# Two short score units in one set of PSUM banks, the product with v in two tasks, and a new order

## The chip, the cores and the metric

The kernel runs on 1 core of one Trainium2 chip. The metric is the device time of one execution in microseconds (us). TensorE (PE) multiplies and transposes into PSUM, VectorE (DVE), ScalarE (ACT) and GpSimd (POOL) do elementwise work, SyncE (SP) issues most DMAs. PSUM is handled here as eight banks of 512 fp32 columns.

## The reference

The inputs are q, k, v of shape (8 batches, 8 heads, 576, 64), a decay f of (8, 8, 576), and an MLP with w1 (512 x 1024) and w2 (1024 x 512), capacity 128.

```
scores = q k^T / 8 + cum[i] - cum[j],  cum = cumsum(log(clip(f)))   # causal
attn   = softmax(scores);  x = attn v, the heads side by side: (8, 576, 512)
per batch: s = x . w_gate;  the 128 rows with the highest s:
   out[row] = x[row] + sigmoid(s[row]) * (relu(x[row] w1) w2);  other rows: out = x
```

## The kernel before

**Pairs and units.** The 64 heads are worked in 32 pairs. q and k are split into a rounded fp32r part and its rest (`rounded`, `rest`), so that the scores are three products; a fourth adds the decay. The causal scores of a pair fall into five units: units 0 to 3 are blocks of 128 queries of either head against 128, 256, 384 and 512 keys, and unit 4 holds the last 64 queries of both heads against all 576. For each unit there is a score task on PE (`s`, line 667, or `s4`, line 735), a mask with a running minimum on DVE (`m`, lines 687, 739), an exponential on ACT (`ex`, lines 692, 747), a turn by 64 x 64 transposes on PE (`tr`, through `turn`, line 352) and two copies of the turned block into `pt` (`cp`; line 335 on ACT, 337 on DVE). A score task takes two banks, one for each head, and a turn task two. Score products and transposes of 64 rows go two at a time, one on the upper and one on the lower rows of the array.

**Product with v.** When all ten copies of a pair are there, one PE task (`av_all`, line 792) runs six pieces, each for both heads, into two neighbouring banks, and one copy of 576 columns takes them to `ot`. `back` turns `ot` (line 352 again, two banks), `norm` divides (line 844), `gate` and `fold` on POOL prepare the gate score (lines 850, 856).

**MLP.** When a batch's gate scores are complete, DVE ranks them (line 999), the 128 rows are gathered by an indirect DMA (line 1054), `xg` (line 1091) forms their gate product again and `xp` turns them; then come the two products (lines 1141, 1182, 1189, 1234, 1242) and a scatter (line 1253). Six of the eight batches are worked two at a time.

**Order.** All tasks are given to a planner (`Flow`) that holds a cost for each and writes the instruction order of every engine. Of the tasks that are ready it takes, on an engine, those whose start lies within `EPS` of the earliest, and among them the one with the smallest `place`, a due time, plus `GW` times the gap that PE is held to need between kinds of tasks. A task with a choice of engines goes where it would end first, with `BD` added for DVE. Tokens stand for buffers; a token "ps" is one bank, or two neighbours. Instructions keep the planned order on their engine, and semaphores order the engines.

```
tks = [Token("ps") for _ in range(2)]          # scores of a unit
tk_t = Token("ps", 2, wide=2)                  # turn of a unit
tk_ot, tk_av = Token("ot", 1), Token("ps", wide=2)
d_xg = add({"dve": 0.7}, xg, after=[q["got"]], place=tx, take=[tk_x])
d_xp = add(turns(ND) ..., xp, after=[d_xg, d_ident], place=tx, ...)
```

Of the kernel before, what the change touches and what calls it, by code (L numbers as in the profile page):

```python
# [17 lines left out]
P = 128  # L18
# [17 lines left out]
class Flow:  # L36
# [18 lines left out]
    def __init__(self, slots, eps, bias, weight, eps0):  # L55
# [122 lines left out]
def kernel(  # L178
# [36 lines left out]
    BD = 0.46  # L215
# [7 lines left out]
    GW = 49.43  # L223
    EPS = 0.05
    EPS0 = 0.21
# [22 lines left out]
    WN = 1  # L248
    Z2 = 2.12
# [3 lines left out]
    OR = 1  # L253
    ORDER = ((3, 0, 2, 1, 4), (4, 3, 0, 2, 1), (3, 2, 4, 1, 0), (3, 2, 1, 0, 4), (0, 3, 2, 1, 4), (4, 3, 2, 1, 0))[OR]
# [25 lines left out]
    sel = const.tile([P, NPAIR], F32R, name="sel")  # L280
    blk = const.tile([P, P], F32, name="blk")
# [93 lines left out]
    def turns(n):  # L375
# [4 lines left out]
                 "oh": 1, "gs": 2}, EPS, {"dve": BD}, GW, EPS0)  # L380
# [154 lines left out]

    def pair_load(p):
# [21 lines left out]
        come = [load(t_b, 295, after=pads, place=pl, take=[tk])]  # L558
        return come + [load(t_a, 295, 3, after=pads + come, place=pl + 0.01)], tk
# [3 lines left out]
    def split_parts(p, come, tk):  # L563
# [24 lines left out]
        if p < HELP1:  # L588
# [3 lines left out]
            rq = part(c1, rounded(qs), after=ready, place=pl)  # L592
            rk = part(c1, rounded(ks), after=ready, place=pl + 0.01)
            lq = part(c2, rest(qs), after=[rq], place=pl + 0.03)
            lk = part(c2, rest(ks), after=[rk], place=pl + 0.04)
# [14 lines left out]
        d_bm[p] = add({"pool": 0.6}, t_bm, after=[d_blk, d_sel] + used4.get(p - 2, []), place=pl)  # L610
# [11 lines left out]
    def pair_parts(p):  # L622
# [13 lines left out]
        lv = load(t_v, 288, 2, rate=300, after=([d_ep] if p == 1 else []) + [d_more[1]] + avd[p - 2:p - 1] * (p > 1), place=9 * p - PV, take=[tk_v])  # L636
# [7 lines left out]
        for u, i in enumerate(ORDER if p else (*(i for i in ORDER if i < NF), NF)):  # L644
            t = 9 * p + 2 * u
            ahead = moved[-LOOK:][:1] if len(moved) >= LOOK else []
            tl = t - LP
            if i < NF:
                n = (i + 1) * P
# [4 lines left out]
                def s(e, k, i=i, n=n, tks=tks, scs=scs, pss=pss):  # L654
                    for par in range(2):
                        if k == 0:
                            scs[par] = bank(tks[par])
                            pss[par] = pw.tile([P, n], F32, tag=f"p{i}", name=f"p{p}_{i}_{par}", bufs=NB[i])
                    cs = [q_cols(p, par, i) for par in range(2)]
                    for m_ in ((0,), (1,), (2,), (3,))[k]:  # L660
                        for par in range(2):
                            h_ = HALVES[par]
                            if m_ == 3:
                                lt, rt = sel[h_, p:p + 1].broadcast_to([R, P]), ep[h_, 0:n]
                            else:
                                lt, rt = q_part(p, m_ == 1)[h_, cs[par]], k_part(p, m_ == 2)[h_, 0:n]
                            nc.tensor.matmul(scs[par][:, :n], lt, rt, start=m_ == 0, stop=m_ == 3)  # L667

                one = max(n / 2400 + 0.014, 0.107) + 0.01
                if p < SPLIT:  # L670
# [3 lines left out]
                    for k in range(4):  # L674
                        x2 = add({"pe": one}, lambda e, k=k, s=s: s(e, k), after=deps[k] + [x2] + (ahead if k == 0 else []),
                                 place=tl + 0.02 * k, take=tks + tks_p if k == 0 else [], kind="score")
                else:
                    x2 = add({"pe": 4 * one}, lambda e, s=s: [s(e, k) for k in range(4)], after=ops[p][0] + ops[p][1] + ahead,
                             place=tl, take=tks + tks_p, kind="score")
                used[p].append(x2)  # L680
                x4s = []
                for par in range(2):
                    tk_nm = Token("nm")

                    def m(e, par=par, n=n, i=i, scs=scs, pss=pss, nms=nms):
                        nm = nms[par] = small.tile([P, 1], F32, tag="nm", name=f"nm{p}_{i}_{par}", bufs=6)
                        nc.vector.tensor_tensor_reduce(  # L687
                            out=pss[par], in0=scs[par][:, :n], in1=mask[:, 512 - n:512], scale=-0.125, scalar=BIG,
                            op0=ALU.add, op1=ALU.min, accum_out=nm)

                    def ex(e, par=par, i=i, pss=pss, nms=nms):
                        nc.scalar.activation(pss[par], pss[par], AF.Exp, bias=nms[par], scale=-1.0,  # L692
                                             accum_out=sts[p % 3][:, i, par:par + 1])

                    x3 = add({"dve": n / 960 + 0.15}, m, after=[x2, d_mask], place=tl + PM + 0.05 * par, take=[tk_nm], give=[tks[par]])
                    x4s.append(add({"act": n / 1200 + 0.295}, ex, after=[x3, d_sums] + d_more[0:1] + invs[p - 3:p - 2] * (p > 2),
                                   place=tl + PE_ + 0.05 * par, give=[tk_nm]))
                sums += x4s
                tk_t = Token("ps", 2, wide=2)

                def tr(e, i=i, tk_t=tk_t, pss=pss):
                    for par in range(2):
                        for j in range(i + 1):
                            turn(tk_t, par * (i + 1) + (j if par == 0 else i - j), pss[par][:, j * P:(j + 1) * P])

                def cp(e, par, i=i, tk_t=tk_t):
# [3 lines left out]
                    copy_on(e, d_, turned(tk_t, par * (i + 1), i + 1))  # L710

                x5 = add(turns(2 * (i + 1)), tr, after=x4s + [d_pt, d_ident], place=t, take=[tk_t], give=tks_p, kind="turn")
                for par in range(2):
                    copied.append(add({**act(n), **dve(n)}, lambda e, par=par, cp=cp: cp(e, par), after=[x5],
                                      place=t + PC + 0.1 * par, give=[tk_t]))
            else:
# [28 lines left out]
                def ex(e):  # L745
# [4 lines left out]
                         take=[tk_b, tk_p], kind="full")  # L750
                used[p].append(x2)
                used4[p] = [x2]
                x3 = add({"dve": S / 960 + 0.15}, m, after=[x2, d_mask4, d_blank], place=tl + U4 + PM, take=[tk_nm], give=[tk_b])
                x4 = add({"act": S / 1200 + 0.295}, ex, after=[x3, d_sums] + d_more[0:1] + invs[p - 3:p - 2] * (p > 2),
                         place=tl + U4 + PE_, give=[tk_nm])
# [13 lines left out]
                x5 = add(turns(NCH), tr, after=[x4, d_pt, d_ident], place=t, take=[tk_t], give=[tk_p], kind="turn")  # L769
                for k in range(2):  # L770
                    w = NCH * R
                    copied.append(add({**act(w), **dve(w)}, lambda e, k=k, cp=cp: cp(e, k), after=[x5],
                                      place=t + PC + 0.1 * k, give=[tk_t]))
# [5 lines left out]
        pieces = ((0, 1), (1, 1), (0, 0), (2, 1), (4, 1), (3, 1))  # L779
        tk_ot, tk_av = Token("ot", 1), Token("ps", wide=2)  # L780
        avs = []
        for n, (j, g) in enumerate(pieces):
            q0 = max(j * P, g * SPL)
            q1 = SPL if g == 0 else S

            def av(e, n=n, j=j, g=g, q0=q0, q1=q1):
                if n == 0:
                    avb[0] = bank(tk_av)
                vt, pt = vts[p], pts[p]
                for par in range(2):  # L790
                    off = (640 * j if par == 0 else 2624 - 512 * j) + q0 - j * P
                    nc.tensor.matmul(  # L792
                        avb[0][par * D:(par + 1) * D, 512 - SPL + q0:512 - SPL + q1],
                        vt[:, j, par * D:(par + 1) * D], pt[:, off:off + q1 - q0],
                        start=(j == 0), stop=(g == 0 or n == len(pieces) - 1))

            avs.append((av, 4 * (q1 - q0)))

        def av_all(e):
            for fn, _ in avs:  # L800
                fn(e)

        x5 = add({"pe": sum(c for _, c in avs) / 2400 + 0.1}, av_all, after=copied + [lv],
                 place=9 * (p + 1) + VO, take=[tk_ot, tk_av], give=[tk_pt, tk_v], kind="av")
        avd.append(x5)

        def out(e):
            copy_on(e, ot[:, 0:S], avb[0][:, 512 - SPL:512 - SPL + S])

# [528 lines left out]
```

## Time and profile before

| | |
|---|---|
| median of 3 runs | 442.49 us (441.96 to 443.34) |
| profiled execution | 440.93 us, its span 439.1 us |
| PE clock granted | 1.00 |
| busy: PE, DVE, ACT, POOL | 400.4, 315.7, 305.0, 278.0 us |

The span runs from the first to the last instruction of the profiled execution. Busy time is the union of an engine's instructions; the ends of matmuls are modelled, so a busy PE is not PE at its peak. "Idle before" in a line is the time in which the engine had nothing to do just ahead of those instructions, and the arrow names what ended it.

### The profile page before, as it was taken

To read this page: it belongs to the slowest core of one execution; us is meant where nothing else is said; L and a number is where in the kernel's file an instruction comes from. 1 tells how busy PE (TensorE), PEld (TensorE's weight loads), DVE (VectorE), ACT (ScalarE), POOL (GpSimd) and SP (SyncE) were. 2 spreads that over 40 slices of the span, in tenths; PEclk is the share of its full clock that TensorE was granted. 3 is DMA by queue.
4 is the path that set the end of the run, shared out by engine and by line. 5 is a ranking of instruction groups with operands and counts; after the bars stand their busy time and mean duration, and the time that the engine had idled before them with its cause. 6 is when DMAs were issued, how large, how long until landed. Compare 5 with 4: busy or idle time off the path is not lost.

```text
span 439.1 us, 12615 instructions
## 1 busy us (share of the span) xinstructions
PE 400.4 (91%) x4649; PEld 317.3 (72%) x4649; DVE 315.7 (72%) x1212; ACT 305.0 (69%) x942; POOL 278.0 (63%) x264
## 2 busy tenths in 40 slices
PE   1999989999889999999999999999999999899995
PEld 1777667777667777798776897777767777698774
DVE  6777777987788876975786738676679787788511
ACT  4799999999889896840588830688879788611310
POOL 4499989999848867952378721568876883310201
PEclk9999999999999999999999999999999999999999
DMA  7965555826443527442134430153536222210201
GB/s 182 269 171 157 134 158 149 222 60 186 125 126 82 160 62 215 139 109 78 52 113 130 137 85 24 52 159 84 150 96 171 80 84 85 53 50 30 73 0 48
DMA packets 43699, 49.82 MB, mean 113 GB/s; under 512 B 6163, under 2 KB 33846, under 8 KB 43638
## 3 DMA queue, kind: packets, MB, share of 16 engines
q1 hardware_dynamic: 42278, 44.68, 36.8%
q0 software_dynamic: 1280, 4.20, 2.9%
q8 instruction: 36, 0.59, 0.6%
q14 instruction: 25, 0.20, 0.2%
q10 hardware_dynamic: 80, 0.15, 0.1%
HBM read 37.45 MB, written 11.55 MB: 112 GB/s over the span
## 4 chain that ended last, share of the span: by engine, by line
ACT 39%; PE 28%; DVE 17%; issue 10%; POOL 2%; DMA 2%; SPq 1%; POOLq 0%; ACTq 0%; DVEq 0%
ACT p L692 20%; ACT pt L335 10%; PE psum L1141 8%; PE psum L667 5%; DVE p L687 5%; PE psum L792 5%; ACT p L747 4%; DVE pt L337 4%; PE psum L1234 4%; DVE j L999 3%; ACT ot L335 3%; PE psum L352 3%; DVE x L844 2%; PE psum L735 2%; PE psum L1242 2%
## 5 line engine op out<-in xcount | busy, mean ns | idle before, releaser
L692 ACT ACTIVATE p<-p,nm 128x512 f32<-128x512 f32 (+3 forms) x256 | 141.1, 559 | 30.9 <-DVE nm L687 30.8
L687 DVE CUSTOM_DVE_ANT_0 p<-psum,mask 128x512 f32<-128x512 f32 (+3 forms) x256 | 110.3, 486 | 7.6 <-PE psum L667 4.1
L667 PE MATMUL psum<-op 64*128 64x512 f32 (+3 forms) x768 | 89.3, 335 | 12.0 <-ACT op L335 9.5
L792 PE MATMUL psum<-pt,v 128*64 128x448 f32 (+4 forms) x768 | 93.8, 393 | 0.2 <-ACT pt L335 0.2
L335 ACT COPY pt<-psum 128x128 f32<-128x128 f32 (+4 forms) x264 | 91.3, 445 | 2.5 <-PE psum L352 2.4
L584 POOL TENSOR_TENSOR op<-raw,op 128x1216 fp32r<-128x1216 f32 (+2 forms) x41 | 88.4, 2165 | 3.0 <-ACT op L335 2.9
L850 POOL TENSOR_TENSOR gp<-x,wg 128x640 f32<-128x640 f32 x31 | 48.9, 1578 | 48.9 <-DVE x L844 46.8
L667 PEld LDWEIGHTS psum<-op 64*128 64x128 f32 x768 | 66.7, 190 | 17.1 <-ACT op L335 9.5
L352 PE MATMUL psum<-ident,p 64*128 64x64 f32 x1600 | 69.3, 228 | 8.3 <-ACT p L747 2.7
L792 PEld LDWEIGHTS psum<-pt,v 128*64 128x64 f32 x768 | 45.4, 137 | 42.9 <-issue 27.8
L352 PEld LDWEIGHTS psum<-ident,p 64*128 64x128 f32 x1600 | 59.4, 139 | 23.4 <-ACT p L692 6.0
L999 DVE TENSOR_SCALAR_CACHE_REDUCE j<-srow,sg 128x128 uint8<-128x128 f32 (+5 forms) x107 | 53.3, 498 | 3.9 <-ACT srow L978 1.3
L337 DVE COPY pt<-psum 128x512 f32<-128x512 f32 (+4 forms) x56 | 27.3, 508 | 35.5 <-ACT pt L335 29.2
L692 ACT ACTIVATION_READ_ACCUMULATOR p<-p,nm 128x1 f32 x256 | 49.9, 195 | 0.0
L856 POOL TENSOR_TENSOR gp<-gp 128x320 f32<-128x320 f32 (+1 forms) x62 | 43.5, 702 | 4.0
L667 PE MATMUL psum<-ep,sel 64*128 64x512 f32 (+3 forms) x256 | 45.0, 324 | 0.0
L577 POOL TENSOR_SCALAR op<-raw 128x1216 fp32r<-128x1216 f32 (+2 forms) x32 | 33.1, 1034 | 7.8 <-PE psum L735 7.3
L335 ACT COPY ot<-psum 128x576 f32<-128x576 f32 x32 | 20.1, 628 | 24.1 <-PE psum L792 24.1
L735 PE MATMUL psum<-op 128*128 128x288 f32 x192 | 34.0, 312 | 1.5 <-DVE nm L687 1.2
L1253 POOL DMA_INDIRECT out_dram<-xe,idx x8 | 8.3, 1034 | 39.2 <-DVE xe L1249 31.0
L735 PEld LDWEIGHTS psum<-op 128*128 128x128 f32 x192 | 26.6, 188 | 5.8 <-DVE nm L687 2.7
L739 DVE CUSTOM_DVE_ANT_0 p<-psum,mask 128x576 f32<-128x576 f32 x32 | 24.2, 756 | 6.5 <-PE psum L735 3.0
(121 smaller groups left out, 597.8 us busy)
## 6 DMA issues: line engine op xcount, KB each, us to landing
raw<-in_qk_dram SPq DMA_DIRECT2D x31, 288.0 KB, 5.4
v<-in_v_dram SPq DMA_DIRECT2D x32, 256.0 KB, 3.0
out_dram<-x SPq DMA_DIRECT2D x16, 512.0 KB, 3.3
raw<-in_qk_dram SPq DMA_DIRECT2D x31, 144.0 KB, 3.3
raw<-in_qk_dram SPq DMA_DIRECT2D x31, 128.0 KB, 3.9
srow<-sd SPq DMA_DIRECT2D x7, 320.0 KB, 4.3
wst<-in_w_dram SPq DMA_DIRECT2D x4, 512.0 KB, 6.6
wst<-in_w_dram SPq DMA_DIRECT2D x8, 256.0 KB, 4.5
```

The costliest lines, as they stand in the source:

```text
L335: nc.scalar.copy(d, s_)
L337: nc.vector.tensor_copy(d, s_)
L352: nc.tensor.transpose(psum[:, o:o + R], src[k_], ident[k_, k_])
L584: (nc.vector if e == "dve" else nc.gpsimd).tensor_tensor(op[:, 1, cs], raw[:, cs], op[:, 0, cs].bitcast(F32), ALU.subtract)
L667: nc.tensor.matmul(scs[par][:, :n], lt, rt, start=m_ == 0, stop=m_ == 3)
L687: nc.vector.tensor_tensor_reduce(out=pss[par], in0=scs[par][:, :n], in1=mask[:, 512 - n:512], scale=-0.125, scalar=BIG, op0=ALU.add, op1=A ...
L692: nc.scalar.activation(pss[par], pss[par], AF.Exp, bias=nms[par], scale=-1.0, accum_out=sts[p % 3][:, i, par:par + 1])
L735: nc.tensor.matmul(sc[:, g * 512:g * 512 + HALF], lt, rt, start=m_ == 0, stop=m_ == 3)
L792: nc.tensor.matmul(avb[0][par * D:(par + 1) * D, 512 - SPL + q0:512 - SPL + q1], vt[:, j, par * D:(par + 1) * D], pt[:, off:off + q1 - q0] ...
L850: (nc.vector if e == "dve" else nc.gpsimd).tensor_tensor(out=st["gp"], in0=x_part(), in1=wg[:, hp * P:(hp + 1) * P].unsqueeze(1).broadcast ...
L856: nc.gpsimd.tensor_tensor(out=g_[:, :, 0:w], in0=g_[:, :, 0:w], in1=g_[:, :, w:2 * w], op=ALU.add)
L999: nc.vector.tensor_scalar(junk[0:n, 0:w, :], src, sg()[0:n, c:c + 1], None, op, ALU.add, accum_out=cnt[0:n, k, c:c + 1])
```

## The change

1. A group of `ORDER` may hold several units. From pair 2 on, units 1 and 0 are one group: one score task writes both into the same two banks (columns 0 to 255 and 256 to 383), one turn task turns both into the same two banks; each keeps its own masks, exponentials and copies. Unit order goes from 4, 3, 0, 2, 1 to 4, 3, 2, (1, 0).
2. The product with v is two tasks with one bank each: queries 0 to 127 (one piece), and 128 to 575 (five pieces). Each has its own copy to `ot`, of 128 and of 448 columns.
3. `xg` writes its unused product to a uint8 tile in SBUF; `xp` no longer comes after `xg` and takes the banks itself.
4. Tasks have a class name `cls`, most of them with a letter for the stage (pairs 0 to 2, 3 to 8, 9 to 26, 27 to 31) or the batch, and a table `SHIFT` adds to the `place` of each class. `BD`, `GW`, `EPS`, `EPS0` are changed.

```
-    BD = 0.46
+    BD = 0.2572
-    GW = 49.43
-    EPS = 0.05
-    EPS0 = 0.21
+    GW = -482.267
+    EPS = 0.0524
+    EPS0 = 0.0601
+    SHIFT = {
+        "ava": 187.02, "avb": -50.46, "avc": -48.88, "avd": 111.42, "bka": -149.68, "bkb": 153.96, "bkc": 129.31,
...
-    ORDER = ((3, 0, 2, 1, 4), (4, 3, 0, 2, 1), ...)[OR]          # OR = 1
+    ORDER = (((4,), (3,), (2,), (1, 0)), ...)[OR]                # OR = 0
...
+        place += self.shift.get(cls, 0.0)
...
-                tks = [Token("ps") for _ in range(2)]
-                tks_p = [Token(f"p{i}") for _ in range(2)]
+                ns = [(i_ + 1) * P for i_ in grp]
+                at = [sum(ns[:k]) for k in range(len(grp))]
+                tks = [Token("ps", len(grp)) for _ in range(2)]
+                tks_p = [Token(f"p{i_}") for i_ in grp for _ in range(2)]
...
+                    for i_, n, a, k in ((*x, k) for x in zip(grp, ns, at) for k in ks):
+                        for par in range(2):
+                            if k == 0:
+                                scs[i_, par] = bank(tks[par])[:, a:a + n]
...
-                tk_t = Token("ps", 2, wide=2)
+                tk_t = Token("ps", 2 * len(grp), wide=2)
-                x5 = add(turns(2 * (i + 1)), tr, after=x4s + [d_pt, d_ident], place=t, take=[tk_t], give=tks_p, kind="turn")
+                x5 = add(turns(2 * sum(ns) // P), tr, after=x4s + [d_pt, d_ident], place=t, take=[tk_t], give=tks_p, kind="turn",
+                         cls="t" + cls)
...
-        pieces = ((0, 1), (1, 1), (0, 0), (2, 1), (4, 1), (3, 1))
-        tk_ot, tk_av = Token("ot", 1), Token("ps", wide=2)
+        tk_ot, tk_av = Token("ot", 1), (Token("ps"), Token("ps"))
+        def av(e, g):
+            if g == 0:
+                avb.update({g_: bank(tk_av[g_]) for g_ in range(2)})
+            js = (0,) if g == 0 else (0, 1, 2, 4, 3)
+            for j in js:
+                q0, q1 = (0, SPL) if g == 0 else (max(j * P, SPL), S)
...
+        def out(e, g):
+            q0, q1 = ((0, SPL), (SPL, S))[g]
+            copy_on(e, ot[:, q0:q1], avb[g][:, 0:q1 - q0])
...
-                    out=q["xp"][0:nr, :], in0=q["xe"][0:nr, :], in1=wg[0:nr, :], scale=1.0, scalar=0.0,
+                    out=junk[0:nr, :], in0=q["xe"][0:nr, :], in1=wg[0:nr, :], scale=1.0, scalar=0.0,
...
-            d_xg = add({"dve": 0.7}, xg, after=[q["got"]], place=tx, take=[tk_x])
-            d_xp = add(turns(ND) if nr == P else pe(256 * ND), xp, after=[d_xg, d_ident], place=tx, ...)
+            d_xg = add({"dve": 0.7}, xg, after=[q["got"]], place=tx, cls=f"xg{b}")
+            d_xp = add(turns(ND) if nr == P else pe(256 * ND), xp, after=[q["got"], d_ident], place=tx, take=[tk_x], ...)
```

## Rows read from the trace of the kernel before

**Rows 1.** The page's first part: busy us, share of the span, instructions.
```profile
PE 400.4 (91%) x4649; PEld 317.3 (72%) x4649; DVE 315.7 (72%) x1212; ACT 305.0 (69%) x942; POOL 278.0 (63%) x264
```

**Rows 2.** The table by stage: stretch, its length, busy us (instructions), clock, DMA.
```profile
0.00:11.00 11.00, 1.53 (x10) 1.44 (x12) 6.89 (x18) 4.97 (x8) 5.23 (x25) 1.00 0.77 182
24.00:50.00 26.00, 23.64 (x324) 17.56 (x325) 17.80 (x61) 25.30 (x79) 25.56 (x23) 1.00 0.56 151
50.00:100.00 50.00, 46.19 (x621) 35.49 (x621) 40.86 (x168) 47.28 (x145) 48.03 (x46) 1.00 0.53 145
300.00:350.00 50.00, 46.99 (x640) 36.15 (x636) 38.14 (x144) 42.65 (x139) 38.64 (x32) 1.00 0.45 121
430.00:439.10 9.10, 3.82 (x17) 2.82 (x15) 0.75 (x1) 0.00 (x0) 0.97 (x1) 0.98 0.10 41
```

**Rows 3.** What PE waited for: us in total, times, longest us.
```profile
PE psum L352 <- DVE pt L337: 7.2, 11, 1.1
PE psum L352 <- ACT pt L335: 3.8, 8, 0.5
...
PE psum L352 <- DVE g L1091: 2.1, 1, 2.1
...
PE psum L667 <- DVE pt L337: 1.1, 2, 0.7
PE psum L667 <- ACT pt L335: 0.8, 3, 0.3
```

**Rows 4.** Timeline of PE, one pair: start us, us, instruction, count.
```profile
309.65 0.94 PE L667 MATMUL psum<-op 64*128 64x512 f32 x6
...
313.62 2.92 PE L792 MATMUL psum<-pt,v 128*64 128x448 f32 x24
316.48 2.02 PE L352 MATMUL psum<-ident,p 64*128 64x64 f32 x50
319.25 0.53 PE L352 MATMUL psum<-ident,ot 64*128 64x64 f32 x10 [0.75 <-DVE pt L337]
319.58 0.94 PE L667 MATMUL psum<-op 64*128 64x512 f32 x6
```

**Rows 5.** Instruction groups by shape, ACT's copies: busy us, mean ns.
```profile
L335 ACT COPY pt<-psum 128x512 f32<-128x512 f32 x48 | 27.0, 603 | 0.0
L335 ACT COPY pt<-psum 128x384 f32<-128x384 f32 x53 | 24.3, 508 | 1.7 <-PE psum L352 1.7
...
L335 ACT COPY ot<-psum 128x576 f32<-128x576 f32 x32 | 20.1, 628 | 24.1 <-PE psum L792 24.1
...
L335 ACT COPY pt<-psum 128x128 f32<-128x128 f32 x55 | 12.7, 290 | 0.4 <-PE psum L352 0.3
```

**Rows 6.** Timeline of ACT, the copies of one pair.
```profile
78.21 3.34 ACT L335 COPY pt<-psum 128x320 f32<-128x320 f32 x10
```

**Rows 7.** Timeline of all engines around a gate product.
```profile
118.34 2.77 POOL L584 TENSOR_TENSOR op<-raw,op 128x1216 fp32r<-128x1216 f32 x1
...
118.64 3.03 DVE L1091 CUSTOM_DVE_ANT_0 psum<-xe,wg 128x512 f32<-128x512 f32 x1
...
121.78 0.46 PE L352 MATMUL psum<-ident,xe 64*128 64x64 f32 x8 [2.10 <-DVE g L1091]
...
122.08 0.79 PE L352 MATMUL psum<-ident,p 64*128 64x64 f32 x20
```

**Rows 8.** Timeline of ACT, the two exponentials of unit 0.
```profile
313.02 0.39 ACT L692 ACTIVATE p<-p,nm 128x128 f32<-128x128 f32 x1
...
313.40 0.39 ACT L692 ACTIVATE p<-p,nm 128x128 f32<-128x128 f32 x1
```

**Rows 9.** What DVE waited for: us in total, times, longest us.
```profile
DVE pt L337 <- ACT pt L335: 29.2, 21, 3.7
```

**Rows 10.** The page's costliest groups: DVE's copies of pt.
```profile
L337 DVE COPY pt<-psum 128x512 f32<-128x512 f32 (+4 forms) x56 | 27.3, 508 | 35.5 <-ACT pt L335 29.2
```

More of the change, by code (lines that the diff above doesn't have):

```diff
@@ L280 @@
     sel = const.tile([P, NPAIR], F32R, name="sel")
+    junk = const.tile([P, 512], U8, name="junk")
     blk = const.tile([P, P], F32, name="blk")
@@ L534, in q_cols, with ph @@
         return slice(o, o + P)
+    def ph(p):
+        return "abcd"[(p > 2) + (p > 8) + (p > 26)]
     def pair_load(p):
@@ L557, in pair_load @@
             pads += ops[p - 2][0] + ops[p - 2][1]
-        come = [load(t_b, 295, after=pads, place=pl, take=[tk])]
-        return come + [load(t_a, 295, 3, after=pads + come, place=pl + 0.01)], tk
+        come = [load(t_b, 295, after=pads, place=pl, take=[tk], cls=f"la{ph(p)}")]
+        return come + [load(t_a, 295, 3, after=pads + come, place=pl + 0.01, cls=f"lb{ph(p)}")], tk
     d_pad0 = []
@@ L591, in split_parts @@
             c2 = {"dve": 0.75} if p == 0 else {"pool": 1.5}
[L592 to L595, printed above, removed]
+            rq = part(c1, rounded(qs), after=ready, place=pl, cls=f"rq{ph(p)}")
+            rk = part(c1, rounded(ks), after=ready, place=pl + 0.01, cls=f"rk{ph(p)}")
+            lq = part(c2, rest(qs), after=[rq], place=pl + 0.03, cls=f"lq{ph(p)}")
+            lk = part(c2, rest(ks), after=[rk], place=pl + 0.04, cls=f"lk{ph(p)}")
             ops[p] = ([rq, rk], [lq, lk])
@@ L598, in split_parts @@
             al = slice(0, QW + S)
-            rq = part({"pool": 1.42}, rounded(al), after=ready, place=pl)
-            lq = part({"pool": 3.0}, rest(al), after=[rq], place=pl + 0.03)
+            rq = part({"pool": 1.42}, rounded(al), after=ready, place=pl, cls=f"rq{ph(p)}")
+            lq = part({"pool": 3.0}, rest(al), after=[rq], place=pl + 0.03, cls=f"lq{ph(p)}")
             ops[p] = ([rq], [lq])
@@ L643, in pair_parts @@
         sums = []
-        for u, i in enumerate(ORDER if p else (*(i for i in ORDER if i < NF), NF)):
+        order = ORDER
+        if p < SPLIT:
+            order = [(i,) for g in ORDER for i in g]
+            if p == 0:
+                order.sort(key=lambda g: g[0] == NF)
+        for u, grp in enumerate(order):
             t = 9 * p + 2 * u
@@ L674, in pair_parts @@
                     for k in range(4):
-                        x2 = add({"pe": one}, lambda e, k=k, s=s: s(e, k), after=deps[k] + [x2] + (ahead if k == 0 else []),
-                                 place=tl + 0.02 * k, take=tks + tks_p if k == 0 else [], kind="score")
-                else:
-                    x2 = add({"pe": 4 * one}, lambda e, s=s: [s(e, k) for k in range(4)], after=ops[p][0] + ops[p][1] + ahead,
-                             place=tl, take=tks + tks_p, kind="score")
+                        x2 = add({"pe": one}, lambda e, k=k, s=s: s(e, (k,)), after=deps[k] + [x2] + (ahead if k == 0 else []),
+                                 place=tl + 0.02 * k, take=tks + tks_p if k == 0 else [], kind="score", cls="s" + cls)
+                else:
+                    x2 = add({"pe": 4 * one}, lambda e, s=s: s(e, range(4)), after=ops[p][0] + ops[p][1] + ahead,
+                             place=tl, take=tks + tks_p, kind="score", cls="s" + cls)
@@ L680, in pair_parts @@
                 used[p].append(x2)
                 x4s = []
[L682 to L697, printed above, removed]
@@ L698, in pair_parts, with m, ex @@
-                sums += x4s
-                tk_t = Token("ps", 2, wide=2)
[L701 to L706, printed above, removed]
+                for i_, n in zip(grp, ns):
+                    for par in range(2):
+                        tk_nm = Token("nm")
+                        def m(e, par=par, n=n, i=i_, scs=scs, pss=pss, nms=nms):
+                            nm = nms[i, par] = small.tile([P, 1], F32, tag="nm", name=f"nm{p}_{i}_{par}", bufs=6)
+                            nc.vector.tensor_tensor_reduce(
+                                out=pss[i, par], in0=scs[i, par], in1=mask[:, 512 - n:512], scale=-0.125, scalar=BIG,
+                                op0=ALU.add, op1=ALU.min, accum_out=nm)
+                        def ex(e, par=par, i=i_, pss=pss, nms=nms):
+                            nc.scalar.activation(pss[i, par], pss[i, par], AF.Exp, bias=nms[i, par], scale=-1.0,
+                                                 accum_out=sts[p % 3][:, i, par:par + 1])
+                        x3 = add({"dve": n / 960 + 0.15}, m, after=[x2, d_mask], place=tl + PM + 0.05 * par, take=[tk_nm],
+                                 give=[tks[par]], cls=f"m{i_}{ph(p)}")
+                        x4s.append(add({"act": n / 1200 + 0.295}, ex, after=[x3, d_sums] + d_more[0:1] + invs[p - 3:p - 2] * (p > 2),
+                                       place=tl + PE_ + 0.05 * par, give=[tk_nm], cls=f"e{i_}{ph(p)}"))
@@ L707, in cp, with tr @@
+                sums += x4s
+                tk_t = Token("ps", 2 * len(grp), wide=2)
+                def tr(e, grp=grp, at=at, tk_t=tk_t, pss=pss):
+                    for i, a in zip(grp, at):
+                        for par in range(2):
+                            for j in range(i + 1):
+                                turn(tk_t, 2 * a // P + par * (i + 1) + (j if par == 0 else i - j), pss[i, par][:, j * P:(j + 1) * P])
+                def cp(e, par, i, a, tk_t=tk_t):
                     dst = pts[p]
@@ L767, in cp @@
                     copy_on(e, d_, turned(tk_t, 0, NCH)[:, :, k, :])
-                x5 = add(turns(NCH), tr, after=[x4, d_pt, d_ident], place=t, take=[tk_t], give=[tk_p], kind="turn")
+                x5 = add(turns(NCH), tr, after=[x4, d_pt, d_ident], place=t, take=[tk_t], give=[tk_p], kind="turn", cls=f"t4{ph(p)}")
                 for k in range(2):
@@ L792, in av @@
                     nc.tensor.matmul(
[L793 to L804, printed above, removed]
+                        avb[g][par * D:(par + 1) * D, q0 - g * SPL:q1 - g * SPL],
+                        vt[:, j, par * D:(par + 1) * D], pt[:, off:off + q1 - q0], start=j == 0, stop=j == js[-1])
+        def out(e, g):
+            q0, q1 = ((0, SPL), (SPL, S))[g]
+            copy_on(e, ot[:, q0:q1], avb[g][:, 0:q1 - q0])
+        wdone = []
+        x5 = None
+        for g, n in ((0, SPL), (1, 448 + 448 + 320 + 64 + 192)):
+            w = (SPL, S - SPL)[g]
+            x5 = add({"pe": 4 * n / 2400 + 0.05}, lambda e, g=g: av(e, g), after=copied + [lv, x5],
+                     place=9 * (p + 1) + VO, take=[tk_ot, *tk_av] if g == 0 else [], give=[tk_pt, tk_v] if g else [], kind="av",
+                     cls=f"av{ph(p)}")
+            wdone.append(add({**act(w), **dve(w)}, lambda e, g=g: out(e, g), after=[x5], place=9 * (p + 1) + VO + 0.2,
+                             give=[tk_av[g]], cls=f"ot{ph(p)}"))
         avd.append(x5)
-        def out(e):
-            copy_on(e, ot[:, 0:S], avb[0][:, 512 - SPL:512 - SPL + S])
-        wdone = [add({**act(S), **dve(S)}, out, after=[x5], place=9 * (p + 1) + VO + 0.2, give=[tk_av])]
         rn, gu = rns[b % 2][:, :, 2 * hp:2 * hp + 2], gus[b % 2]
@@ L822, in pair_parts @@
         gt = gates[b]
-        d_inv = add({"dve": 0.45}, inv, after=sums + invs[-1:], place=bp - 2, take=[gt["tk"]] if hp == 0 and NRT else [])
+        d_inv = add({"dve": 0.45}, inv, after=sums + invs[-1:], place=bp - 2, take=[gt["tk"]] if hp == 0 and NRT else [], cls=f"in{ph(p)}")
         invs.append(d_inv)
@@ L862, in gsum @@
                 axis=mybir.AxisListType.X, op=ALU.add)
-        x6 = add(turns(NCH), back, after=wdone, place=bp, take=[tk_b], give=[tk_ot], kind="turn")
-        n0 = add({"dve": 0.82}, norm, after=[x6, d_inv], place=bp + 0.3, take=[nk["tk"]] if w_ == 0 else [], give=[tk_b])
+        x6 = add(turns(NCH), back, after=wdone, place=bp, take=[tk_b], give=[tk_ot], kind="turn", cls=f"bk{ph(p)}")
+        n0 = add({"dve": 0.82}, norm, after=[x6, d_inv], place=bp + 0.3, take=[nk["tk"]] if w_ == 0 else [], give=[tk_b], cls=f"no{ph(p)}")
         nk["done"].append(n0)
@@ L1028, in moe_parts @@
         ts = t0 + RK + RD * NCH
-        x = moe_sel[b] = add({"dve": 0.12}, sel0, after=ranks + [d_more[2]], place=ts, give=[tk_srow, gates[b]["tk"]] + ([tk_dg] if end else []))
-        sels = [add({"dve": NRT * 0.133 + 0.2}, lambda e, c=c: sel(e, c), after=[x], place=ts + 0.1 * c) for c in range(NCH)]
+        x = moe_sel[b] = add({"dve": 0.12}, sel0, after=ranks + [d_more[2]], place=ts, give=[tk_srow, gates[b]["tk"]] + ([tk_dg] if end else []), cls=f"se{b}")
+        sels = [add({"dve": NRT * 0.133 + 0.2}, lambda e, c=c: sel(e, c), after=[x], place=ts + 0.1 * c, cls=f"se{b}") for c in range(NCH)]
         for rt in range(NRT):
@@ L1056, in gd @@
                 in_offset=bass.IndirectOffsetOnAxis(ap=q["idx"][0:nr, 0:1], axis=0))
-        x = add({"pe": 0.4}, ga, after=sels, place=tg, take=[tk_i], give=[tk_oh] if tk_oh else [], kind="full")
+        x = add({"pe": 0.4}, ga, after=sels, place=tg, take=[tk_i], give=[tk_oh] if tk_oh else [], kind="full", cls=f"gi{b}")
         x = add({"dve": 0.07}, ix, after=[x], place=tg + 0.1, give=[tk_i])
-        q["got"] = add({"pool": 1.04}, gd, after=[x] + stored[b], place=tg - 5, take=[tk_xe], lat=3.2)
+        q["got"] = add({"pool": 1.04}, gd, after=[x] + stored[b], place=tg - 5, take=[tk_xe], lat=3.2, cls=f"gd{b}")
         return q
@@ L1118, in gr @@
                 nc.vector.reciprocal(q["g"][0:nr], q["g"][0:nr])
-            d_xg = add({"dve": 0.7}, xg, after=[q["got"]], place=tx, take=[tk_x])
-            d_xp = add(turns(ND) if nr == P else pe(256 * ND), xp, after=[d_xg, d_ident], place=tx, kind="turn" if nr == P else "full")
+            d_xg = add({"dve": 0.7}, xg, after=[q["got"]], place=tx, cls=f"xg{b}")
+            d_xp = add(turns(ND) if nr == P else pe(256 * ND), xp, after=[q["got"], d_ident], place=tx, take=[tk_x], kind="turn" if nr == P else "full", cls=f"xp{b}")
             d_xh.append(add({"act": 0.478}, xh, after=[d_xp] + d_xh[:1], place=tx, take=[tk_xh] if g == 0 else [], give=[tk_x]))
@@ L1146, in group_parts @@
                                    place=tp + gs * k, take=[tk_a] if s_ == m_ == 0 else [],
-                                   give=[tk_xh] if m_ < 2 else [tk_xh, tk_xl], kind="full")
+                                   give=[tk_xh] if m_ < 2 else [tk_xh, tk_xl], kind="full", cls=f"l1{name[0]}")
                         k += 1
@@ L1184, in group_parts @@
                     prev = add(pr(512, 2), g1, after=d_xh + [d_w[c], prev], place=tp + gs * k,
-                               take=[tk_a] if c == 0 else [], give=[tk_xh], kind="full")
+                               take=[tk_a] if c == 0 else [], give=[tk_xh], kind="full", cls=f"l1{name[0]}")
                     k += 1
@@ L1190, in g1l @@
                                          start=False, stop=(c == ND - 1))
-                    prev = add(pr(512), g1l, after=d_xl + [prev], place=tp + gs * (k - 0.4 + 0.1 * c), give=[tk_xl], kind="full")
+                    prev = add(pr(512), g1l, after=d_xl + [prev], place=tp + gs * (k - 0.4 + 0.1 * c), give=[tk_xl], kind="full", cls=f"l1{name[0]}")
                 def relu(e, n=n):
@@ L1236, in group_parts @@
                 prev = add(pr(512, 2), g2, after=[hhs[c], d_w[ND + c], prev], place=tp + gs * (k + 1),
-                           take=[tk_y] if c == 0 else [], give=[tk_hh[c // CT]], kind="full")
+                           take=[tk_y] if c == 0 else [], give=[tk_hh[c // CT]], kind="full", cls=f"l2{name[0]}{qs.index(q)}")
                 k += 1
@@ L1244, in group_parts @@
                         prev = add(pr(512), g2l, after=[hls[d_], prev], place=tp + gs * (k + 0.6 + 0.1 * (d_ % 4)),
-                                   give=[tk_hl[d_ // CT]], kind="full")
+                                   give=[tk_hl[d_ // CT]], kind="full", cls=f"l2{name[0]}{qs.index(q)}")
             def fin(e, q=q, nr=nr):
```

88 lines of the change are left out of this document (46 added, 42 removed), and 19 rows, old and new, of the table SHIFT.

## The prediction

> **What bounds the kernel now.** I read the busy shares first, then the table by stage, then what PE waited for, then one pair of heads line by line. TensorE (PE) is busy for 400.4 us and ScalarE (ACT) for 305.0 [rows 1]; nothing else comes near PE over the whole span. The table by stage says where PE is not busy [rows 2]: 9.47 us before the first operands exist (0 to 11), 5.28 us behind the last product (430 to 439.1), and the rest, 439.1 - 400.4 - 9.47 - 5.28 = 24 us, in the middle, where it is spread: 2.4 us of the 26 from 24 to 50, 3.8 of the 50 from 50 to 100, 3.0 of the 50 from 300 to 350. In the first two of these ACT itself has no room (25.30 of 26.00, 47.28 of 50.00); in the last it has 7.4 us.
>
> Who ends those 24 us is in the waits of PE [rows 3]. Four of the five rows name a copy of turned probabilities (pt) out of PSUM: 7.2 + 3.8 + 1.1 + 0.8 = 12.9 us, some 24 waits. The waiting instruction writes PSUM and does not read pt, so these are waits for a bank to come free. One wait of 2.1 us is on the gate product g.
>
> One pair shows it [rows 4]. All scores run from 309.65 to 313.62, the product of the pair before with v (AV) to 316.48, then 50 transposes that stretch over 2.02 us, then 0.75 us of nothing, then the turn of ot, and at 319.58 the next pair begins: a period of 9.93 us. Transposes go two at a time, and the ten of ot take 319.58 - 319.25 = 0.33 us, 0.066 a couple; 25 couples would take 1.65. So this pair loses 0.75 + 0.37 = 1.1 us to copies that hold banks.
>
> **The change part by part.** The number of matmuls does not change, nor their shapes: score, turn and AV columns are the same. So the 400 us of PE work stay, and all that can be won is in the 24 us and in stretched phases that count as busy.
>
> *Banks.* Before, a pair claims 24 banks in sequence: two for the scores and two for the turns of each of five units, two for AV, two for the turn of ot. After, units 1 and 0 go together (2 + 2 instead of 4 + 4), so 20; and AV's two banks are freed one by one. The claim that waits most, the turn of ot, is the last of the turn phase: it was the sixth couple of banks in a row and becomes the fifth, and PSUM has four (8 banks); so it still needs a release, but an earlier one. The most that goes is the whole 12.9 us; the least is nothing, or below it if the shared banks are held longer than the two they replace (the slower rival below). I take half, **-6.5 us**: of the two claims over the four couples one goes and one remains. Late next is PE itself at some points, and at others ACT's first exponential of the pair, which waits for the first mask.
>
> *AV in two tasks.* The same six pieces, the 128 queries first. Instead of one copy of 576 columns, 628 ns, there are copies of 128 and 448 [rows 5]: 290 ns and, between 508 (384) and 603 (512), 556. That is 218 ns more a pair on ACT if both stay there. Over 32 pairs it is 7.0 us, but ACT has room in most stages; where it has not (24 to 100, some 8 pairs at 9.93 us) it is on the path: 8 x 0.218 = **+1.7 us**. Nothing, if DVE takes one of the two (it now can, each bank being its own); 7.0 if ACT turns out to set the pace everywhere. Behind the copies only the turn of ot waits, and that has a whole pair's time.
>
> *Which engine copies.* BD is the extra cost that the planner puts on DVE when it chooses who copies; it falls from 0.46 to 0.2572. At 78.21 ACT takes ten pt copies in a row, 3.34 us [rows 6], 0.33 each, while it is the full engine. If DVE takes two more of the ten in those 8 pairs, 8 x 2 x 0.33 = 5.3 us less on ACT; at worst nothing, or a loss where the masks stand behind the copy on DVE (a mask of 512 delayed by one copy). I take under a third, **-1.6 us**.
>
> *Gate product xg.* It wrote into the banks that the turn of xe uses, so the turn waited for it. Now it writes junk in SBUF and the turn waits only for the gathered rows. At 118.64 xg took 3.03 us, beside a POOL subtraction of 2.77 us that began at 118.34 and shares its end, and PE stood 2.1 us [rows 7]. After, PE can run the turn of xe and the 20 transposes behind it in that hole, 0.46 + 0.79 = **-1.2 us**; at most the 2.1, at least nothing, because xg still stands on DVE and the mask behind it comes no sooner. No other wait of PE names g. The Trainium skill ("SBUF — State Buffer", Who interferes with whom) says a DVE operation with two SBUF inputs and a GpSimd operation exclude each other for a whole instruction; the row of 3.03 us agrees, and by it this part keeps DVE late as often as before, and a term of 0 would give 1.2 us more time.
>
> *Order.* SHIFT and GW change which of several ready tasks goes first. They act only among tasks whose start lies within EPS, 0.05 us, of the earliest, so PE is not held for a favoured task. That removes no work; the remaining 24 - 12.9 - 2.1 = 9 us of middle idle are what it could win, and the same 9 what a worse order could lose, as I see no reason for a sign. **0, between -9 and +9.** Loads are shifted too (SP's queue, POOL's roundings): they are hidden as long as raw is two pairs ahead.
>
> *Merged unit's added wait.* Its turn waits for four exponentials where unit 1's waited for two. The two more are of 128 columns, and one such costs 0.38 us from its start to the next, the accumulator read between included [rows 8]: two are 0.77. Behind this turn stand on PE its copies' consumer AV and the turn of ot. AV of a pair runs after the next pair's scores (309.65 to 313.62, 4 us), so 0.77 is covered as long as the scores are not themselves late: **0**, at most 0.77 a pair.
>
> Sum: -6.5 + 1.7 - 1.6 - 1.2 = -7.6 us. The profiled execution took 440.93 us (span 439.1 and 1.83 around it): 433.3. The median of the runs shown, 442.49, lies 1.56 us above it, so **434.9 us** for the runs.
>
> **The rivals.**
> *A: the waits go and something else stands there (442 us).* The first exponential of a pair waits for the first mask, which waits for the scores; if PE's lost 1.1 us only moves ahead of ACT, nothing is won. For it: ACT has no room from 24 to 100. Against it: 7.4 us of room from 300 to 350, with the same 0.75 us hole. Bank gain 0, and -1.6 - 1.2 + 1.7 = -1.1: about 441.4 to 442.5.
>
> *B: the shared banks serialise (slower, 446.6 us).* DVE's pt copies stood idle 29.2 us, 21 times, until an ACT pt copy ended [rows 9], although both only read the turned block: two engines are not let into one bank at once. With two units in one couple of banks four copies queue instead of two, and the 0.77 us of later turn comes first. Some 22 of the 32 pairs run outside the stretches that MLP products fill (16 from 24 to 182 us at 9.93, 6 from 300 on; an estimate). If 0.77 is exposed in each, 22 x 0.77 = 16.9; the bank waits that do go, 22 x 0.5 = 11, and xg's 1.2 are set against it, and a longer queue of copies of nothing more: +4.7, less 0.6 for the copies DVE takes: 446.6. It decides this way when the merged unit's copies end later than the next pair's scores and u4, 4 us after they begin. The Trainium skill ("PSUM — Partial Sum Buffer", PSUM bank collisions raise a hardware error) has it as a rule that no two engines may touch one bank and quadrant at a time; the row of 29.2 us agrees, and it is the rule that speaks against sharing.
>
> *C: the turn phase comes apart (420 us).* If four couples of banks let turns of one pair run between scores of the next, the whole 1.1 us goes in the 22 pairs: 24 us, less 1.7: 442.49 - 22 = 420. For it: the holes have one cause. Against it: ten copies in a row on ACT are 3.34 us whatever the banks are.
>
> **How the numbers follow.** The likeliest case, 434.9, has 0.55, and its own range is 427 to 441 (bank term 0 to 12.9). A has 0.12, B 0.21, C 0.12. The likeliest and C are faster than 442.49 by over 0.3% (1.3 us, about what a measurement of this kernel can tell from no change): 0.67. A is the same: 0.12. B is slower: 0.21. For eight in ten the range goes down to 424.5, leaving out most of C, and up to 446, leaving out half of B.
>
> **What would show it.** Right: pt rows in the waits of PE sum to about 6 us; the turn of ot follows the transposes with less than 0.4 us between; the pair's period near 9.5; more pt copies on DVE than 56 [rows 10]; the row of g gone from PE's waits. Wrong: ACT near full from 300 to 350 with no fewer holes on PE (A); transposes that wait for the exponentials of units 0 and 1 (B); PE busy under 390 us in the same number of matmuls, with the period under 9 (C). If the middle idle grows by rows that name neither copies nor exponentials, the order did it, and the term I set to 0 was the one that mattered.

## The result, and the profile after

The changed kernel takes 428.62 us (median of 4 runs, 428.38 to 431.34), the kernel before 442.76 in the same measurement; the ratio is 0.9696 (95% interval 0.966 to 0.9732). That is 14.1 us less; 7.6 were forecast.

The profiled execution took 431.34 us, its span 429.6. The first line of the page of after, against [rows 1]:

```profile
PE 397.9 (93%) x4649; PEld 313.6 (73%) x4649; DVE 325.7 (76%) x1234; ACT 302.3 (70%) x952; POOL 278.0 (65%) x264
```

The matmuls are as many as before. What PE waited for (us in total, times, longest), against [rows 3]:

```profile
PE psum L390 <- DVE pt L375: 5.3, 10, 1.6
PE psum L715 <- DVE pt L375: 2.7, 7, 0.7
PE psum L390 <- ACT pt L373: 1.9, 6, 0.5
PE psum L715 <- ACT pt L373: 1.8, 5, 0.7
```

The four pt rows sum to 11.7 us, where they were 12.9: read alone, the banks seem to have won almost nothing. Two things hide there. The waits have moved from the transposes (line 390, 11.0 to 7.2) to the scores (line 715, 1.9 to 4.5). And a wait between two transposes of one run is short and counts as busy. So the groups by shape have to be read (busy us, mean ns, idle us before them), first of before, then of after:

```profile
L352 PE MATMUL psum<-ident,p 64*128 64x64 f32 x1600 | 69.3, 228 | 8.3 <-ACT p L747 2.7 <-DVE pt L337 2.7 <-ACT p L692 0.5
...
L352 PE MATMUL psum<-ident,ot 64*128 64x64 f32 x320 | 16.8, 229 | 8.1 <-DVE pt L337 4.5 <-ACT pt L335 3.5
```
```profile
L390 PE MATMUL psum<-ident,p 64*128 64x64 f32 x1600 | 63.6, 226 | 6.5 <-DVE pt L375 3.0 <-DVE xtl L1160 1.5 <-ACT pt L373 1.1
...
L390 PE MATMUL psum<-ident,ot 64*128 64x64 f32 x320 | 16.7, 228 | 3.6 <-DVE pt L375 2.3 <-ACT pt L373 0.8 <-DVE xtl L1160 0.2
```

The same 1600 transposes are busy 5.7 us less, and the idle time before both groups falls from 16.4 to 10.1. That is 12.0 us in the turn phase (the transposes and the idle time before them). Not all of it is banks: 2.7 us of the idle time before were two waits for unit 4's exponential (`ACT p L747`), and after has none. The pt waits fell by 3.8 us there, the stretch by 5.7, and the scores give 2.6 of pt waits back, so the banks won at most 3.8 + 5.7 - 2.6 = 6.9 us. That most of the 5.7 are bank waits too shows in the steps from one transpose to the next that took over 90 ns without counting as idle: 118 in before, 68 in after, and the end of a pt copy released PE or its weight load in 58 of them before and in 17 after.

One cycle of after, against [rows 4]:

```profile
147.49 1.77 PE L390 MATMUL psum<-ident,p 64*128 64x64 f32 x50
149.18 0.52 PE L390 MATMUL psum<-ident,ot 64*128 64x64 f32 x10
149.83 0.63 PE L715 MATMUL psum<-op 64*128 64x256 f32 x6
...
153.83 2.92 PE L844 MATMUL psum<-pt,v 128*64 128x128 f32 x24
156.68 1.77 PE L390 MATMUL psum<-ident,p 64*128 64x64 f32 x50
...
158.97 0.61 PE L715 MATMUL psum<-op 64*128 64x256 f32 x6
```

The turns take 1.77 us instead of 2.02, the turn of ot follows at once, and the cycle is 156.68 - 147.49 = 9.19 us, where the one shown of before was 9.93. Single cycles scatter, so like stages are set side by side: from one turn of ot to the next, before took 8.89 to 10.36 us in the six pairs from 299.96 us on, 9.75 on average, and after 8.92 to 9.60 in the five from 316.66 on, 9.31 on average.

This profiled execution is the longest of the four, and the granted clock says why. The stages around 304 us (length, busy of PE, PEld, DVE, ACT, POOL, then the clock):

```profile
300.00:303.40 3.40, 1.81 (x54) 1.64 (x52) 2.75 (x6) 1.99 (x9) 2.54 (x2) 1.00 0.48 117
303.40:312.00 8.60, 8.24 (x64) 7.01 (x66) 4.99 (x18) 5.07 (x16) 6.56 (x5) 0.60 0.40 127
```

After a wait of 1.59 us for a pt copy PE ran 8.6 us at 0.60 on average, so mostly at 1.2 GHz instead of 2.4. The scores and u4 of that pair took 6.9 us (304.61 to 311.50), against 3.97 in [rows 4]: 2.9 us, about the distance to the fastest run.

At the two ends of the span PE stands about as long as in [rows 2]:

```profile
0.00:11.00 11.00, 1.73 (x12) 1.63 (x14) 6.57 (x18) 5.17 (x8) 5.58 (x28) 1.00 0.74 184
420.50:429.60 9.10, 3.80 (x17) 2.81 (x15) 0.75 (x1) 0.00 (x0) 0.97 (x1) 0.86 0.10 40
```

So PE's idle time in the middle is 429.6 - 397.9 - 9.27 - 5.30 = 17.1 us, where the prediction counted 24. These 6.9 us less, with the 2.5 that PE is busy less in spite of the low clock, make up 9.4 of the 9.5 us between the two spans. The low clock hides 2.9 us more, and the profiled execution of before (440.93 us) lies 1.8 us below its median: together about the 14.1.

### The profile page after: what moved, and what is told of

It is laid out like the page before. It is cut to its first block, busy times and chain, and to the rows that moved or that the text cites. A ratio compares the mean times of both kernels' runs of the same rounds, so it can differ in the third digit from the quotient of the medians.

```text
span 429.6 us, 12712 instructions
## 1 busy us (share of the span) xinstructions
PE 397.9 (93%) x4649; PEld 313.6 (73%) x4649; DVE 325.7 (76%) x1234; ACT 302.3 (70%) x952; POOL 278.0 (65%) x264
## 4 chain that ended last, share of the span: by engine, by line
PE 37%; ACT 32%; issue 14%; DVE 12%; DMA 2%; POOL 1%; POOLq 0%; SPq 0%; ACTq 0%; DVEq 0%
ACT p L742 16%; ACT pt L373 10%; PE psum L715 9%; PE psum L844 8%; PE psum L1191 7%; DVE pt L375 4%; PE psum L789 4%; PE psum L1284 4%; PE psum L390 3%; ACT p L801 3%; ACT ot L373 2%; DVE x L895 2%; DVE p L737 2%; PE psum L1292 2%; DMA raw<-in_qk_dram 2%
## 5 line engine op out<-in xcount | busy, mean ns | idle before, releaser
L742 ACT ACTIVATE p<-p,nm 128x128 f32<-128x128 f32 (+3 forms) x256 | 142.1, 564 | 23.5 <-DVE nm L737 23.4
L715 PE MATMUL psum<-op 64*128 64x384 f32 (+3 forms) x768 | 90.2, 340 | 14.9 <-ACT op L373 9.3
L626 POOL TENSOR_TENSOR op<-raw,op 128x1216 fp32r<-128x1216 f32 (+2 forms) x41 | 90.8, 2219 | 1.9 <-ACT op L373 1.7
L373 ACT COPY pt<-psum 128x256 f32<-128x256 f32 (+4 forms) x249 | 87.2, 445 | 5.5 <-DVE pt L375 3.5
L390 PE MATMUL psum<-ident,p 64*128 64x64 f32 x1600 | 63.6, 226 | 6.5 <-DVE pt L375 3.0
L390 PEld LDWEIGHTS psum<-ident,p 64*128 64x128 f32 x1600 | 56.1, 139 | 18.5 <-issue 4.9
L375 DVE COPY pt<-psum 128x512 f32<-128x512 f32 (+4 forms) x71 | 33.1, 500 | 32.9 <-ACT pt L373 29.0
L715 PE MATMUL psum<-ep,sel 64*128 64x384 f32 (+3 forms) x256 | 45.5, 329 | 0.0
L373 ACT COPY ot<-psum 128x448 f32<-128x448 f32 (+1 forms) x59 | 23.4, 396 | 26.5 <-PE psum L844 26.1
L715 PEld LDWEIGHTS psum<-ep,sel 64*128 64x128 f32 x256 | 28.3, 195 | 1.1
```

What stands on the lines that cost most here:

```text
L373: nc.scalar.copy(d, s_)
L375: nc.vector.tensor_copy(d, s_)
L390: nc.tensor.transpose(psum[:, o:o + R], src[k_], ident[k_, k_])
L626: (nc.vector if e == "dve" else nc.gpsimd).tensor_tensor(op[:, 1, cs], raw[:, cs], op[:, 0, cs].bitcast(F32), ALU.subtract)
L715: nc.tensor.matmul(scs[i_, par], lt, rt, start=k == 0, stop=k == 3)
L742: nc.scalar.activation(pss[i, par], pss[i, par], AF.Exp, bias=nms[i, par], scale=-1.0, accum_out=sts[p % 3][:, i, par:par + 1])
```

## The experiments

Two questions had to be kept apart: what the edits are worth, and what the order is worth that the planner makes of them. Each edit gives a new plan, and a plan is a draw. So variants of the tasks were given the same 90 drawn sets of BD, GW, EPS and EPS0, without SHIFT, and of each variant the set with the shortest plan was run (its own "first of 90"); two more kept the old order by force. "New gate product" is the edit of `xg` and `xp`. All ratios are to the kernel before on the same chip: 442.22 us beside e1 to e4, 443.11 beside e5 to e8, 442.27 beside e9 to e12. The expectations name theories by letters of their own: their A and B are not the rivals A and B of the prediction.

| run | shared | product with v | settings | us | ratio (95%) |
|---|---|---|---|---|---|
| e1 | none | one task | old, EPS 0.045 | 472.55 | 1.0679 (1.0637 to 1.072) |
| e2 | both | two | old, no SHIFT | 450.0 | 1.0193 (1.0119 to 1.0266) |
| e3 | both | one | first of 90 | 434.3 | 0.9833 (0.9797 to 0.9869) |
| e4 | none | two | first of 90 | 442.72 | 1.002 (1.0001 to 1.0038) |
| e5 | none | one | first of 90 | 439.45 | 0.9933 (0.9902 to 0.9964) |
| e6 | turns | one | first of 90 | 436.78 | 0.9857 (0.9833 to 0.9881) |
| e7 | scores | one | first of 90 | 440.09 | 0.9941 (0.9923 to 0.9958) |
| e8 | both | two | first of 90 | 424.7 | 0.9587 (0.9556 to 0.9618) |
| e9 | both | one | second of 90 | 436.95 | 0.9884 (0.9845 to 0.9924) |
| e10 | both | two | the set of e9 | 434.1 | 0.9804 (0.9765 to 0.9843) |
| e11 | none | one | old order held, new gate product | 441.88 | 0.999 (0.9961 to 1.0018) |
| e12 | none | two copies | old order held | 442.64 | 1.001 (0.9991 to 1.0028) |

**e1, another order of the old tasks.**

```
-    EPS = 0.05
+    EPS = 0.045
```


> The kernel before with EPS 0.045 in place of 0.05 and nothing else, so the same tasks and banks in another order. Theory S (shared banks give the turns room between the next pair's scores, and that is the gain): no order of the old tasks comes near 428.6; this one is a draw at 440 to 455, and in the stretch 70 to 110 us the turns of a pair stay in one run, with a period of 9.5 us or more. Theory O (the order alone is the gain, the sharing is not needed): the draw may fall anywhere from 428 to 455.

472.55 us, beyond what either theory had. A tie window a tenth narrower costs 30 us. What PE waited for there:

```profile
PE psum L352 <- ACT p L747: 16.4, 13, 1.9
PE psum L667 <- ACT op L335: 9.4, 1, 9.4
PE psum L1045 <- DVE oh L1025: 8.1, 1, 8.1
```

PE's next transposes are those of unit 4, whose exponential is not done, 13 times; and 8.1 us at the end stand on the last batch's selection. PE is also busy for 411.7 us, 11.3 more than in [rows 1] for as many matmuls, at a mean clock of 0.966.

**e2, the three edits under the old settings.**

```
-    BD, GW, EPS, EPS0 = 0.2572, -482.267, 0.0524, 0.0601
-    SHIFT = {"ava": 187.02, ...}
+    BD, GW, EPS, EPS0 = 0.46, 49.43, 0.05, 0.21
+    SHIFT = {}
```


> The changed kernel with SHIFT empty and BD, GW, EPS, EPS0 as before: the three edits of the code without the tuned order. S: faster than 442.5, about 434 to 438. O: 442 or slower. A (the product with v in two tasks is what helps): also faster, 434 to 438.

450 us: slower than before, as theory O had it. But the loss sits in the tail. From 395 us on PE waited:

```profile
PE psum L1063 <- DVE oh L1043: 9.1, 1, 9.1
PE psum L357 <- DMA xe<-out_dram,idx: 3.9, 1, 3.9
```

This order has done its MLP work early and has nothing left to put under the last batch's selection and gather, so this run says little about the turn phase.

**e3 and e4, one edit each.**

```
e3:  pieces = (...); tk_av = Token("ps", wide=2); one av task, one copy
e4:  if True: order = [(i,) for g in ORDER for i in g]     # no group; units 4, 3, 2, 1, 0
```


> Shared banks and the new gate product, the product with v in one task of two banks as before, no SHIFT; BD, GW, EPS, EPS0 are the best of 90 drawn sets by the length of the planner's own plan. S: 428 to 434, with turns between the next pair's scores. O: 438 or slower, since the tuned order is gone. A: 438 or slower.

> No shared banks; the product with v in two tasks and the new gate product, no SHIFT; BD, GW, EPS, EPS0 the best of the same 90 drawn sets. S: 437 to 446, no gain beyond 1 per cent. A: 428 to 434. O: like e3 within 2 us.

434.3 and 442.72, 0.3 us above the range that S had for e3 and inside the one for e4: in these two draws the gain comes with the shared banks, and the split without them is worth nothing. S holds on that, and O, which had them within 2 us of each other, does not. The other half of S falls: the turns are no more mixed with scores than before. Counted in the traces, PE goes from transposes of p to scores or u4 21 times in before, 22 in after, 20 in e3, and 103 times in e4, where the transposes of p are busy 78.1 us.

**e5 to e8, which of the banks.**

```
e5:  no group, order 4, 3, 2, 1, 0
e6:  tks = {i_: [Token("ps") ...] for i_ in grp}, a score task each; tk_t = Token("ps", 2 * len(grp), wide=2)
e7:  tks = [Token("ps", len(grp)) ...]; a turn task and a tk_t for each unit
e8:  all edits, SHIFT = {}, BD, GW, EPS, EPS0 = 0.3, 19.2, 0.0572, 0.162
```


> Nothing shared, one product task, new gate product, unit order 4, 3, 2, 1, 0, no SHIFT; the best of the same 90 drawn planner sets. If sharing is worth the 8 us between e4 and e3, this lies at 441 to 449, beside e4. If e3 was a lucky draw, it lies within 3 us of 434.

> As e5, but units 1 and 0 share one turn task and its two banks; their scores keep banks of their own. Theory T (the turn phase, where ot waits for a couple of banks, carries the gain): 434 to 437. Theory Q (the scores, ten banks before and eight after, carry it): 441 to 446. Theory B (a pair fits into eight banks only with both): 438 to 444.

> As e5, but units 1 and 0 share one score task and its two banks; their turns keep tasks and banks of their own. T: 441 to 446. Q: 434 to 437. B: 438 to 444.

> Both shared and the product with v in two tasks, all edits of the change, no SHIFT, the best of the same 90 sets. If the split is worth nothing by itself: 432 to 437, like e3. If it is part of the gain: 431 or less, so that little is left for SHIFT.

Nothing shared gives 439.45, the turns alone 436.78, the scores alone 440.09, both 434.3. That is T's order, and Q is out; but e5 fell between its two ranges, e7 0.9 us below T's and inside B's, and 2.7 us between two draws are thin. e8 was the surprise: 424.7 us, faster than the changed kernel. Its last pairs have another cycle:

```profile
329.51 1.40 PE L357 MATMUL psum<-ident,p 64*128 64x64 f32 x38
330.72 0.93 PE L682 MATMUL psum<-op 64*128 64x512 f32 x6
...
331.72 0.53 PE L357 MATMUL psum<-ident,p 64*128 64x64 f32 x12
332.06 0.77 PE L682 MATMUL psum<-op 64*128 64x384 f32 x6
...
333.72 0.49 PE L357 MATMUL psum<-ident,ot 64*128 64x64 f32 x10
...
335.39 2.92 PE L811 MATMUL psum<-pt,v 128*64 128x128 f32 x24
338.25 1.40 PE L357 MATMUL psum<-ident,p 64*128 64x64 f32 x38
```

The scores of 512 keys stand between the turns, the others before the turn of ot, and no transpose waits in this cycle. The cycle is 338.25 - 329.51 = 8.74 us, and the stage from 300 to 350 has no room left on PE nor on ACT, against 46.99 and 42.65 in [rows 2]:

```profile
300.00:350.00 50.00, 49.78 (x699) 38.24 (x700) 40.01 (x164) 49.32 (x167) 38.76 (x32) 1.00 0.44 125
```

**e9 and e10, another draw.** Both with `BD, GW, EPS, EPS0 = 0.47, -5.2, 0.0527, 0.108`, e9 on the tasks of e3 and e10 on those of e8.

> The tasks of e3 under another of the 90 drawn sets (BD 0.47, EPS 0.0527, EPS0 0.108, GW -5.2), the second by the length of its plan. If e3's 434.3 belongs to the tasks: 431 to 438. If single draws scatter by 10 us and more, as e1 and e2 suggest: anywhere from 425 to 450.

> The tasks of e8 under the same set as e9. If the split is worth what lies between e8 and e3: 8 to 11 us less than e9, with the cycle turn, score, turn, score in the last pairs. If e8 was a lucky order: within 4 us of e9.

436.95 and 434.1: 2.9 us for the split, not ten, which by the expectation makes e8 a lucky order. e3 and e9 lie 2.7 us apart, e8 and e10, with the same tasks, 9.4. PE goes from transposes of p to scores 69 times in e8 and 35 times in e10.

**e11, the new gate product in the old order.**

```
-                    out=q["xp"][0:nr, :], ...    xp, after=[d_xg, d_ident]
+                    out=junk[0:nr, :], ...       xp, after=[q["got"], d_ident], take=[tk_x]
```


> The order of the kernel before, instruction by instruction, with the gate product in SBUF and the turn of xe no longer behind it. The prediction's term: 1.2 us less, with the 2.1 us row gone from PE's waits. Against it: 0, because DVE's mask behind the gate product comes no sooner.

The interval of the ratio holds 1, and the timeline, against [rows 7], shows where the 2.1 us went:

```profile
118.71 2.79 POOL L698 TENSOR_TENSOR op<-raw,op 128x1216 fp32r<-128x1216 f32 x1
...
118.83 3.22 DVE L1204 CUSTOM_DVE_ANT_0 junk<-xe,wg 128x512 uint8<-128x512 f32 x1
...
119.89 0.41 PE L466 MATMUL psum<-ident,xe 64*128 64x64 f32 x8
...
120.62 0.59 PE L466 MATMUL psum<-ident,p 64*128 64x64 f32 x12 [0.32 <-ACT pt L449]
...
122.72 0.46 PE L466 MATMUL psum<-ident,p 64*128 64x64 f32 x8 [1.51 <-DVE nm L801]
```

The turn of xe goes ahead, and 2.8 us later PE waits 1.51 us for the mask that stands behind the gate product on DVE. The Trainium skill ("SBUF — State Buffer", Who interferes with whom) says that a DVE instruction with two SBUF inputs contends with a GpSimd instruction that reads SBUF. The traces agree: the gate product took 3.22 us here beside a POOL operation of 2.79, and a median of 0.69 us over the eight batches. The uint8 target in SBUF did not change that: with the target in PSUM it was 3.03 us beside 2.77 [rows 7].

**e12, two copies in the old order.**

```
-            copy_on(e, ot[:, 0:S], avb[0][:, 512 - SPL:512 - SPL + S])
+            copy_on(e, ot[:, 0:SPL], avb[0][:, 0:SPL])
+            copy_on(e, ot[:, SPL:S], avb[0][:, 512:512 + S - SPL])
```


> The order of the kernel before, with the product with v in two banks that do not hold parts of each other and two copies (128 and 448) one behind the other on the engine that had the one of 576. The prediction's term: 1.7 us more. If ACT set the pace: 7 more. If the copies are hidden: 0.

0.4 us more, interval 0.4 less to 1.2 more: the second copy is hidden. (The product is still one task here, and both copies run on the engine that had the one copy.) The groups on ACT, against 20.1 us for the copies of 576 in [rows 5]:

```profile
L448 ACT COPY ot<-psum 128x448 f32<-128x448 f32 x32 | 17.0, 531 | 7.9 <-PE psum L905 7.9
...
L448 ACT COPY ot<-psum 128x128 f32<-128x128 f32 x32 | 8.0, 250 | 15.0 <-PE psum L905 15.0
```

## Why the prediction was right

It was right in direction and about half the size (7.6 us of 14.1). By its steps:

- **Banks, -6.5.** The place was right, and the size, at most 6.9, came near by luck. The prediction halved the visible pt waits, and these fell by 1.2 us over all (-3.8 at the transposes, +2.6 at the scores). The 5.7 us came from the stretch, which it had worked out itself for one pair (0.37) and left out of the sum. Its test, pt rows of about 6 us, would have failed a change that worked; the cycle (9.31 on average for "near 9.5") was the better test.
- **AV in two, +1.7.** Two copies measured +0.4 with the order held, and the interval does not hold 1.7: the copy is covered even where ACT is nearly full. By itself it wins nothing either (e4, e12); with shared banks 2.9 us in one pair of draws (e10 against e9), and how much more in a good order is open.
- **Which engine copies, -1.6.** The direction is right: 71 pt copies on DVE for 56 [rows 10], and ACT's busy time falls 2.7 us in spite of the split. Its worth alone was not measured.
- **Gate product, -1.2.** The row of g, 2.1 us, is gone from PE's waits, as forecast; with the order held the edit measured -0.4, and the interval, 1.7 less to 0.8 more, holds both 0 and the forecast. The reason given against it, the mask behind it on DVE, is what the trace shows.
- **Order, 0 between -9 and +9.** This is the step that failed as an argument. The code's tie rule does bound how long PE is held for one task, but not what follows: e1 shows +30 us for the old tasks, and the new tasks run from 424.7 to 450. In after itself the 2.7 us of waits on unit 4's exponential are gone, for which only this 0 had room. SHIFT is not needed: without it the same tasks took 424.7 and 434.1 under drawn settings, on either side of 428.62.
- **Merged unit's wait, 0.** It held: in after, PE's waits on exponentials of units 0 to 3 sum to 0.4 us.

Rival B fell on its price: DVE's pt copies stood 29.0 us behind ACT's, 26 times, for 29.2 and 21 in [rows 9]. The Trainium skill ("PSUM — Partial Sum Buffer", PSUM bank collisions raise a hardware error) has it that two engines cannot access the same bank of a partition at the same time. The trace agrees in that DVE's copies wait for ACT's, but in total they queue no longer with two units in a couple of banks than with one:

```profile
DVE pt L375 <- ACT pt L373: 29.0, 26, 3.6
```

Rival A is out by the time and by the cycle. Rival C, the turn phase coming apart, is not what after does in its plain cycles, but it is what e8 does, at 8.74 us a pair. Coming apart is not enough by itself: in e4 and e5, with nothing shared, PE goes from transposes to scores 103 and 109 times, at 442.72 and 439.45 us.

Is the sharing the cause? With settings from the same 90 sets the kernels with both shared took 434.3, 436.95, 424.7 and 434.1, those with nothing shared 439.45 and 442.72. All four lie below both. The traces show where: the transposes of p and ot, busy and idle before them together, take 84.3 to 92.1 us in the seven kernels whose turns share banks (after, e2, e3, e6, e8, e9, e10) and 97.1 to 109.8 in the seven whose turns do not (before, e1, e4, e5, e7, e11, e12), whatever the order; e2 has 90.3 although it took 450 us. What of this reaches the time depends on the order: draws scatter by 9 us, so the size, some 2.5 to 18, stays open. That the old tasks have no better order was not shown; with nothing shared only one draw of each variant was run.

## What to carry to other kernels

Count what a buffer ring is asked for in one phase: one claim less over four couples of banks won up to 6.9 us although the waits that the profile named fell by 1.2, because waits inside a run of short instructions count as busy. Where a planner writes the order, undoing an edit and planning again measures a draw: hold the order for the price of an edit, and compare several draws for the worth of a structure. The best kernel here, e8, has all edits and no SHIFT: 424.7 us.

## What was not expected of the hardware

PE fell to a mean clock of 0.60 for 8.6 us behind a wait of 1.59 us in after, while behind the 2.1 us wait of before [rows 7] the clock stayed at 1.00. What else it takes is open. In e1, with many such waits, the mean clock over the span was 0.966.
